# Loading q, k and v head by head in 1 KB pieces, and turning them by fp32 matmuls in blocks of 64 columns

## The chip, the cores and the metric

The kernel runs on one core of a Trainium2 chip. The metric is the device time of one execution in microseconds, the median of several runs. The engines of the core are TensorE (PE in the profile; its weight loads are shown apart as PEld), VectorE (DVE), ScalarE (ACT), GpSimd (POOL) and SyncE (SP, which here only issues DMAs). They run their own instruction lists in order and wait for one another by semaphores.

## The reference

Attention that keeps the 32 largest scores of each row, and behind it a feed-forward layer with a squared ReLU. The shapes are 8 batches, 8 heads, 576 rows, 64 columns for q, k and v, and 512 to 2048 to 512 for the layer; all inputs and the output are fp32.

```
scores = q @ k.T / 8                                  # per batch and head, 576 x 576
kth    = 32nd largest of each row
attn   = exp(scores - max) where scores >= kth, else 0; each row divided by its sum
x      = attn @ v                                     # heads put side by side: 4608 x 512
out    = relu(x @ w_in) ** 2 @ w_out
```

## The kernel before

**Tiling.** Two heads of one batch make a pair; there are 32 pairs. The 576 rows of a head are cut into 4 chunks of 128 (row `4 p + c` stands on partition `p` of chunk `c`) and a remainder of 64. A step `u` handles 128 query rows of two heads at once, against all 576 keys; the remainders of two pairs share two steps. There are 144 steps, in an order written out in `steps`.

**One step.** TensorE makes the scores in two banks of 2 x 288 columns, `sc_a` and `sc_b` (L263, fp32; the two heads of a pair sit on partitions 0 to 63 and 64 to 127 and use the upper and the lower rows of the array). ScalarE copies both banks to `s` (L266). VectorE takes pairwise maxima out of the banks and of `s` (L282, L283, and L285 in the first 20 steps), then maxima and minima of these (L291, L292), and in four rounds the 8 largest values and their removal (L342, L346). From step 20 on VectorE writes one of the pairwise results into the bank `sc_b`, ScalarE copies it out to `most` (L298), and L291 and L292 follow. L292 is the last reader of bank `sc_b`, so the next step's scores for that bank come after it. GpSimd builds the remaining candidates (L307, L316) and a mask (L378), which from step 20 on a DMA issued by GpSimd adds to `s` (L382, `s<-gone`). ScalarE takes the exponentials (L386), a transposing DMA on SyncE's queue turns them (L395, `wT<-w_two`), TensorE multiplies by v (L422), VectorE inverts the row sums (L436), ScalarE scales the result into `x_tok` or `x_rem` (L452, L459). Between these TensorE does pieces of the feed-forward layer, `dense` (L533, L556; L572 are idle pieces), which ScalarE evacuates (L538, L544, L561).

**Preparing a pair.** Each pair has a list of units, `prep_units`: `main` for q, `main` for k, `rest`, `values`. A unit `main` turns the four chunks of two heads with four 128-column transposes of TensorE into one bank `gen` (L161), and ScalarE copies it to `qkT` (L162), for q with the scale. `rest` turns the remainders (L197) and copies them (L199, L200, L202). `values` copies v into bf16 (L206, L209). The first pair is cut up in `first_step` and `first_q` so that the first scores come early. In the main loop one unit is issued per step (two in the first 8 steps, no unit in a step that keeps `values` for later): TensorE's list has it right behind the step's scores, ScalarE's list right behind the copies of these scores.

The order of a step around the change:

```
scores(u + 1)
both(u + 1)
...
prepare(u)
place(u - 4)
exps(u - 2, 0); exps(u - 2, 1); turn(u - 2)
fetch(10 if u < 8 else 3)
topk(u, (1, 2))
pairs_of(u + 1); copy_far(u + 1); lesser(u + 1)
topk(u, (3,))
```

ScalarE's list thus runs: copies of the scores (L266), the copy of a prepared unit (L162 or others), L452 or L459, the exponentials (L386), then `most` (L298), then the feed-forward evacuations.

**Loading.** `load_pair` puts a pair's ten loads into a list, and `fetch` issues them from it on SyncE's queue, ten per step in the first 8 steps and then three: for each of q, k and v one load for each head (L104, rows 0 to 511, 128 KB) and one for the remainder of both (L109, 32 KB), for v twice. The tile is `[128, 5, 2, 64]`: chunk, head, column, so that a chunk of both heads is a run of 128 columns for the transpose, and each load writes pieces of 64 fp32 (256 bytes). The tiles have two buffers. `load_first` does the same for the first pair on SyncE's and ScalarE's queues (L131, L134).

Of the kernel before, what the change touches and what calls it, by code (L numbers as in the profile page):

```python
# [13 lines left out]
f32 = mybir.dt.float32  # L14
# [4 lines left out]
AF = mybir.ActivationFunctionType  # L19
# [4 lines left out]
def kernel(  # L24
# [9 lines left out]
    nc = tc.nc  # L34
# [10 lines left out]
    def pin(ins):  # L45
        tc.keep_in_program_order(ins)
        return ins
# [3 lines left out]
    ld = fast.enter_context(tc.tile_pool(name="ld", bufs=2))  # L51
# [9 lines left out]
    id_f = const.tile([128, 128], f32, name="id_f")  # L61
# [30 lines left out]
    raw, prep = {}, {}  # L92

    fetches = []

    def load_pair(i):
        b, pr = pairs[i]
        raw[i] = [None] * 3

        def whole_rows(z, name, two, a):  # L100
            def go():
                if a == 0:
                    raw[i][z] = ld.tile([128, 5, 2, 64], f32, name=name)
                pin(nc.sync.dma_start(out=raw[i][z][:, 0:4, a, :], in_=two[a, 0:512].rearrange("(p c) d -> p c d", c=4)))  # L104
            return go

        def rest_rows(z, two, at):
            def go():
                pin(nc.sync.dma_start(out=raw[i][z][at:at + 64, 4], in_=two[:, 512:576].rearrange("h p d -> p h d")))  # L109
            return go  # L110

        for z, (name, src) in enumerate((("q_raw", q), ("k_raw", k), ("v_raw", v))):
            two = src[b, 2 * pr:2 * pr + 2]
            for a in range(2):
                fetches.append((i, whole_rows(z, name, two, a)))
            fetches.append((i, rest_rows(z, two, 0)))
            if z == 2:
                fetches.append((i, rest_rows(z, two, 64)))

    def fetch(n):  # L120
        while n and fetches:
            fetches.pop(0)[1]()
            n -= 1


    def load_first():
        raw[0] = [ld.tile([128, 5, 2, 64], f32, name=name) for name in ("q_raw", "k_raw", "v_raw")]
        at = [z[0, 0:2] for z in (q, k, v)]

        def rows(queue, z, a):  # L130
            pin(queue.dma_start(out=raw[0][z][:, 0:4, a, :], in_=at[z][a, 0:512].rearrange("(p c) d -> p c d", c=4)))  # L131

        def last(queue, z, to=0):
            pin(queue.dma_start(out=raw[0][z][to:to + 64, 4], in_=at[z][:, 512:576].rearrange("h p d -> p h d")))  # L134

        for z in (1, 0):
            rows(nc.sync, z, 0)
            rows(nc.scalar, z, 1)
        last(nc.sync, 1)
        last(nc.scalar, 0)  # L140
        rows(nc.sync, 2, 0)
        rows(nc.sync, 2, 1)
        last(nc.sync, 2)
        last(nc.sync, 2, 64)

    def prep_units(i):
        q_raw, k_raw, v_raw = raw[i]
        qkT = heads.tile([128, 512 + 640], f32, name="qkT")
        qT, kT = qkT[:, 0:512], qkT[:, 512:1152]
        k_rest = kT.rearrange("p (n d) -> p n d", d=64)[:, 0:10:9]  # L150
        bd, va = qbd[i % 5], vau[i % 6]
        prep[i] = (qT, kT, bd, va)

        def twice(t):
            return t.rearrange("p (o d) -> p o d", o=1).broadcast_to([128, 2, 64])

        def main(which, src):
            def go():
                tp = ps_one.tile([128, 512], f32, name="gen", bufs=2)
                for c in range(4):  # L160
                    pin(nc.tensor.transpose(tp[:, c * 128:(c + 1) * 128], src[:, c], id_f[:, :]))  # L161
                pin(nc.scalar.activation((qT, kT[:, 64:576])[which], tp[:, :], AF.Copy, scale=(scale, 1.0)[which]))  # L162
            return go


        def first_step():
            for j, bank in ((0, "gen"), (1, "gen"), (2, "dn_ps"), (3, "sc_a")):
                if bank == "sc_a":
                    tp = ps_sc.tile([128, 2, 512], f32, name=bank)[:, 0, :]
                else:  # L170
                    tp = ps_one.tile([128, 512], f32, name=bank, bufs=2 if bank == "gen" else None)
                if j < 2:
                    for c in range(2):
                        pin(nc.tensor.transpose(tp[:, c * 128:(c + 1) * 128], k_raw[:, 2 * j + c], id_f[:, :]))
                    to, got = kT[:, 64 + j * 256:64 + (j + 1) * 256], tp[:, 0:256]
                elif j == 2:
                    pin(nc.tensor.transpose(tp[:, 0:128], q_raw[:, 0], id_f[:, :]))
                    to, got = qT[:, 0:128], tp[:, 0:128]
                else:
                    pin(nc.tensor.transpose(tp[:, 0:64], k_raw[0:64, 4], id_f[0:64, 0:64]))  # L180
                    to, got = k_rest, twice(tp[:, 0:64])
                if j % 2:
                    pin(nc.vector.tensor_copy(to, got))
                else:
                    pin(nc.scalar.activation(to, got, AF.Copy, scale=scale if j == 2 else 1.0))

        def first_q():
            tp = ps_one.tile([128, 512], f32, name="gen", bufs=2)
            for c in range(1, 4):
                pin(nc.tensor.transpose(tp[:, c * 128:(c + 1) * 128], q_raw[:, c], id_f[:, :]))  # L190
            pin(nc.scalar.activation(qT[:, 128:512], tp[:, 128:512], AF.Copy, scale=scale))

        def rest(both=(0, 1)):
            tp = ps_one.tile([128, 512], f32, name="gen", bufs=2)
            for which in both:
                src = (q_raw, k_raw)[which]
                pin(nc.tensor.transpose(tp[:, which * 64:(which + 1) * 64], src[0:64, 4], id_f[0:64, 0:64]))  # L197
            if 0 in both:
                pin(nc.scalar.activation(bd[0:64, 0:64], tp[0:64, 0:64], AF.Copy, scale=scale))  # L199
                pin(nc.scalar.activation(bd[64:128, 64:128], tp[64:128, 0:64], AF.Copy, scale=scale))  # L200
            if 1 in both:
                pin(nc.scalar.activation(k_rest, twice(tp[:, 64:128]), AF.Copy))  # L202

        def values():
            assert i < 6 or av_left[i - 6] == 0
            pin(nc.scalar.activation(va[:, 0:4, :, 0:64], v_raw[:, 0:4], AF.Copy))  # L206
            for x in range(2):
                half = slice(64 * x, 64 * x + 64)
                pin(nc.scalar.activation(va[half, 4 + x, :, 0:64], v_raw[half, 4], AF.Copy))  # L209
# [418 lines left out]


    load_first()  # L630
    load_pair(1)
    fetch(10)
    soon, coming = prep_units(0), 1
    soon.pop(0)()

# [34 lines left out]
    def ok(w):  # L670
        return 0 <= w < U
# [16 lines left out]
    for u in range(U):  # L688
        for x in range(2):
            if ok(u - 1) and not by_vector(u - 1, x):  # L690
                drop(u - 1, x)
        quads_of(u)
        topk(u, (0,))
        if ok(u - 4):
            invert(u - 4)
        if ok(u + 1):
            for i, c, a in steps[u + 1]:
                while coming <= i or (coming == i + 1 and soon):
# [198 lines left out]
```

## Time and profile before

| | us |
|---|---|
| median of the runs | 942.67 |
| lowest, highest of 3 | 941.9, 949.06 |
| the profiled execution | 951.19 |
| its span, first to last instruction | 949.4 |
| busy TensorE, weight loads | 685.4, 413.2 |
| busy VectorE | 897.8 |
| busy ScalarE | 785.9 |
| busy GpSimd | 777.3 |

The profile comes from one execution. A row of the timeline gives start and duration in us, engine, line, operation, output and input, and how many instructions were merged; in brackets stands how long the engine was idle before it and for whom it waited. A row of the list of waits gives engine and line, whom it waited for, the total in us, how often, and the longest. A row of the groups gives the count, then busy us and mean ns, then idle time before the group. A row of the windows gives the window, its length, busy time and count of each engine, and last the clock granted to TensorE, the busy share of the DMA engines and GB/s.

### The profile page before, as it was taken

What the parts mean: (1) busy time and instruction counts of PE and PEld (TensorE: products, weight loads), DVE (VectorE), ACT (ScalarE), POOL (GpSimd) and SP (SyncE); (2) the same over time, 40 slices, a digit from 0 to 9 for tenths busy, and PEclk for the clock granted to TensorE, in tenths of its full rate; (3) what the DMA queues carried; (4) which work ended last, traced back from release to release, by engine and by line L of the source; (5) the groups of instructions that cost most, each with busy time, mean ns of one, the idle gap of its engine ahead of it and who ended that gap; (6) DMA issues with size and microseconds to landing.
All of it is one profiled execution on the core that took longest, in us unless ns stands there. A gap on an engine that the chain in (4) does not pass through costs nothing.

```text
span 949.4 us, 19099 instructions
## 1 busy us (share of the span) xinstructions
PE 685.4 (72%) x5264; PEld 413.2 (44%) x5264; DVE 897.8 (95%) x3635; ACT 785.9 (83%) x1778; POOL 777.3 (82%) x803
## 2 busy tenths in 40 slices
PE   6777677777677777667766677777777777688766
PEld 3333344445354434344544434444544443455544
DVE  5999999999899999999979999999999999999971
ACT  4677897888698979798969888889899987988982
POOL 7888889887788898988878888888888888898850
PEclk9998988997889999998879999999899999998999
DMA  5667866898999999989899999898999999687741
GB/s 138 131 157 173 172 131 131 180 195 183 175 189 177 193 218 185 208 180 192 189 150 194 191 205 212 185 197 185 193 204 198 196 199 214 141 174 159 159 110 38
DMA packets 329969, 166.16 MB, mean 175 GB/s; under 512 B 306560, under 2 KB 306560, under 8 KB 329856
## 3 DMA queue, kind: packets, MB, share of 16 engines
q1 hardware_dynamic: 311088, 92.62, 51.3%
q0 software_dynamic: 17568, 71.97, 33.3%
q8 instruction: 44, 0.72, 0.3%
q14 instruction: 69, 0.57, 0.2%
q10 hardware_dynamic: 1200, 0.30, 0.1%
HBM read 37.75 MB, written 9.44 MB: 50 GB/s over the span
## 4 chain that ended last, share of the span: by engine, by line
DVE 49%; issue 10%; ACT 7%; DMA 7%; POOL 5%; PE 4%; SPq 0%; POOLq 0%; ACTq 0%
DVE m L342 20%; DVE cat L346 14%; DMA s<-gone_b 5%; DVE sc_b L282 4%; DVE cat L291 4%; DVE cat L292 4%; DVE most L283 3%; PE dn_ps L556 2%; DMA s<-gone_a 1%; PE gen L533 1%; POOL cat L316 1%; POOL gone_b L378 1%; POOL gone_a L378 1%; ACT w_two_c L386 1%; DVE rsum L436 1%
## 5 line engine op out<-in xcount | busy, mean ns | idle before, releaser
L342 DVE MAX8 m<-cat 128x8 f32<-128x104 f32 (+3 forms) x1152 | 446.9, 430 | 0.0
L346 DVE MATCH_REPLACE8 cat<-m,cat 128x104 f32<-128x104 f32 (+2 forms) x864 | 270.7, 322 | 0.0
L307 POOL TENSOR_TENSOR cat<-s 128x576 int32<-128x576 int32 (+1 forms) x144 | 230.5, 1601 | 2.9 <-ACT s L266 2.9
L316 POOL TENSOR_TENSOR cat<-cat,most 128x576 int32<-128x576 int32 (+1 forms) x144 | 190.2, 1321 | 28.6 <-ACT most L298 8.8
L263 PE MATMUL sc_b<-qkT 64*128 64x288 f32 x512 | 108.1, 497 | 125.3 <-DVE cat L292 123.5
L556 PE MATMUL dn_ps<-w_out,h 128*128 128x512 bf16 x576 | 162.0, 417 | 3.6 <-ACT wide L561 3.6
L533 PEld LDWEIGHTS <-w_in 128*128 128x128 bf16 x1408 | 126.6, 105 | 70.1 <-issue 38.2
L533 PE MATMUL gen<-xT,w_in 128*128 128x256 bf16 (+1 forms) x1120 | 140.2, 277 | 15.4 <-ACT qkT L202 5.9
L266 ACT ACTIVATE s<-sc_b 128x576 f32<-128x576 f32 x144 | 93.3, 648 | 61.4 <-PE sc_b L263 60.5
L378 POOL TENSOR_SCALAR gone_b<-s,neg 128x576 uint8<-128x576 f32 x142 | 106.0, 746 | 32.5 <-ACT neg L361 22.9
L378 POOL TENSOR_SCALAR gone_a<-s,neg 128x576 uint8<-128x576 f32 x143 | 106.7, 746 | 29.4 <-ACT neg L361 20.6
L263 PE MATMUL sc_a<-qkT 64*128 64x288 f32 x512 | 102.6, 477 | 31.0 <-DVE most L283 21.0
L263 PEld LDWEIGHTS sc_b<-qkT 64*128 64x128 f32 x512 | 46.8, 205 | 177.9 <-issue 95.7
L266 ACT ACTIVATE s<-sc_a 128x576 f32<-128x576 f32 x144 | 91.6, 636 | 11.5 <-PE sc_a L263 10.5
L422 PEld LDWEIGHTS <-wT 128*128 128x128 bf16 (+1 forms) x1600 | 61.7, 102 | 85.3 <-DMA wT<-w_two_b 31.9
L538 ACT ACTIVATE rl<-gen 128x512 f32<-128x512 f32 x142 | 84.7, 597 | 12.6 <-PE gen L533 12.1
L544 ACT ACTIVATE h<-rl 128x512 bf16<-128x512 f32 x138 | 86.9, 630 | 4.4
L556 PEld LDWEIGHTS <-h 128*128 128x128 bf16 x576 | 56.1, 105 | 70.6 <-issue 32.9
L386 ACT ACTIVATE w_two_c<-s,neg 128x576 bf16<-128x576 f32 x94 | 68.0, 780 | 16.0 <-DMA s<-gone_b 12.1
L291 DVE TENSOR_TENSOR cat<-sc_b,most 128x288 f32<-128x288 f32 x144 | 63.8, 443 | 13.4 <-ACT most L298 13.2
L386 ACT ACTIVATE w_two_b<-s,neg 128x576 bf16<-128x576 f32 x95 | 68.8, 780 | 3.9 <-DMA s<-gone_b 2.4
L382 POOL DMA_DIRECT2D s<-gone_b x61 | 54.2, 888 | 20.1 <-DVE cat L346 7.4
(165 smaller groups left out, 1202.0 us busy)
## 6 DMA issues: line engine op xcount, KB each, us to landing
s<-gone_a POOLq DMA_DIRECT2D x61, 576.0 KB, 4.7
s<-gone_b POOLq DMA_DIRECT2D x61, 576.0 KB, 4.7
v_raw<-in_v_dram SPq DMA_DIRECT2D x64, 128.0 KB, 3.2
out_dram<-wide SPq DMA_DIRECT2D x32, 256.0 KB, 2.7
k_raw<-in_k_dram SPq DMA_DIRECT2D x63, 128.0 KB, 3.3
q_raw<-in_q_dram SPq DMA_DIRECT2D x63, 128.0 KB, 3.0
wide<-in_moe_w_in_dram SPq DMA_DIRECT2D x8, 512.0 KB, 4.3
wide<-in_moe_w_out_dram SPq DMA_DIRECT2D x8, 512.0 KB, 4.2
```

The lines of the kernel that those rows point to most:

```text
L263: pin(nc.tensor.matmul(out=ps[j][:, x, 0:HALF], lhsT=lhsT, rhs=rhs, start=True, stop=True))
L266: pin(nc.scalar.activation(s[:, :, j * HALF:(j + 1) * HALF], ps[j][:, :, 0:HALF], AF.Copy))
L291: pin(tt(cat[:, :, 0:QUAR], far, near, op=ALU.max))
L307: pin(tt(less, s[:, :, 0:wide].bitcast(i32), s[:, :, HALF:HALF + wide].bitcast(i32), op=ALU.add))
L316: pin(tt(less, less, d["most"][:, 0:n_h, :, :].bitcast(i32).rearrange("p h x n -> p x h n"), op=ALU.subtract))
L342: pin(nc.vector.max(out=m[r][:, x, :], in_=part(r, x)))
L346: pin(nc.vector.match_replace(out=part(r, x), in_to_replace=m[r][:, x, :], in_values=part(r, x), imm_value=NEG))
L378: pin(nc.gpsimd.tensor_scalar(byte[:, x, :, 1], s[:, x, :], scalar1=d["neg"][:, x, 1:2], scalar2=-HUGE, op0=ALU.add, op1=ALU.mult))
L386: pin(nc.scalar.activation(w_two[u % 3][:, x, 0:S], d["s"][:, x, :], AF.Exp, bias=d["neg"][:, x, 0:1]))
L533: pin(nc.tensor.matmul(out=hp[:, n * n_rows:(n + 1) * n_rows], lhsT=w_in[:, kh, (f0 + n) * 128:(f0 + n + 1) * 128], rhs=xt(kh), start=(kh ...
L544: pin(nc.scalar.activation(h2, flat, AF.Square))
L556: pin(nc.tensor.matmul(out=op[:, :], lhsT=held["h2"][:, f, c * 128:(c + 1) * 128], rhs=w_out[:, f, :], start=(f == 0), stop=(f == NF - 1)))
```

## The change

The tile of raw rows becomes `[128, 640]`: on each partition first the 4 rows of one head (256 columns, 1 KB), then those of the other, then 128 columns for the remainder of both. One load now brings rows 0 to 511 of both heads, and its pieces are 1 KB long, on both sides. A pair has seven loads; `fetch` issues seven in the first steps and then two. The first pair's loads keep their number and their queues and are 1 KB in their pieces as well.

A chunk of both heads is no longer one run of columns. The new function `flip` turns it by two ordinary fp32 matmuls: the 64 columns of one head are the weights, the identity is the moving operand (128 columns), and the results go to partitions 0 to 63 and 64 to 127 of the bank. `main`, `first_step` and `first_q` use it. The remainders keep the transpose. `values` reads v in another order.

```
+    def rest_of(t, at):
+        return t[at:at + 64, 512:640].rearrange("p (h d) -> p h d", h=2)
+
+    def flip(to, t, c):
+        for a in range(2):
+            pin(nc.tensor.matmul(out=to[64 * a:64 * a + 64, :], lhsT=t[:, 256 * a + 64 * c:256 * a + 64 * c + 64], rhs=id_f[:, :], start=True, stop=True))
...
-        def whole_rows(z, name, two, a):
+        def whole_rows(z, name, two):
             def go():
-                if a == 0:
-                    raw[i][z] = ld.tile([128, 5, 2, 64], f32, name=name)
-                pin(nc.sync.dma_start(out=raw[i][z][:, 0:4, a, :], in_=two[a, 0:512].rearrange("(p c) d -> p c d", c=4)))
+                t = raw[i][z] = ld.tile([128, 640], f32, name=name)
+                pin(nc.sync.dma_start(out=t[:, 0:512].rearrange("p (h x) -> p h x", h=2), in_=two[:, 0:512].rearrange("h (p c) d -> p h (c d)", c=4)))
...
-            pin(queue.dma_start(out=raw[0][z][:, 0:4, a, :], in_=at[z][a, 0:512].rearrange("(p c) d -> p c d", c=4)))
+            pin(queue.dma_start(out=raw[0][z][:, 256 * a:256 * a + 256], in_=at[z][a, 0:512].rearrange("(p c) d -> p (c d)", c=4)))
...
                 for c in range(4):
-                    pin(nc.tensor.transpose(tp[:, c * 128:(c + 1) * 128], src[:, c], id_f[:, :]))
+                    flip(tp[:, c * 128:(c + 1) * 128], src, c)
                 pin(nc.scalar.activation((qT, kT[:, 64:576])[which], tp[:, :], AF.Copy, scale=(scale, 1.0)[which]))
...
-            pin(nc.scalar.activation(va[:, 0:4, :, 0:64], v_raw[:, 0:4], AF.Copy))
+            pin(nc.scalar.activation(va[:, 0:4, :, 0:64], v_raw[:, 0:512].rearrange("p (a c d) -> p c a d", a=2, c=4), AF.Copy))
...
-    fetch(10)
+    fetch(7)
...
-        fetch(10 if u < 8 else 3)
+        fetch(7 if u < 8 else 2)
```

More of the change, by code (lines that the diff above doesn't have):

```diff
@@ L108, in go @@
             def go():
-                pin(nc.sync.dma_start(out=raw[i][z][at:at + 64, 4], in_=two[:, 512:576].rearrange("h p d -> p h d")))
+                pin(nc.sync.dma_start(out=rest_of(raw[i][z], at), in_=two[:, 512:576].rearrange("h p d -> p h d")))
             return go
@@ L113, in load_pair @@
             two = src[b, 2 * pr:2 * pr + 2]
-            for a in range(2):
-                fetches.append((i, whole_rows(z, name, two, a)))
+            fetches.append((i, whole_rows(z, name, two)))
             fetches.append((i, rest_rows(z, two, 0)))
@@ L126, in load_first @@
     def load_first():
-        raw[0] = [ld.tile([128, 5, 2, 64], f32, name=name) for name in ("q_raw", "k_raw", "v_raw")]
+        raw[0] = [ld.tile([128, 640], f32, name=name) for name in ("q_raw", "k_raw", "v_raw")]
         at = [z[0, 0:2] for z in (q, k, v)]
         def rows(queue, z, a):
-            pin(queue.dma_start(out=raw[0][z][:, 0:4, a, :], in_=at[z][a, 0:512].rearrange("(p c) d -> p c d", c=4)))
+            pin(queue.dma_start(out=raw[0][z][:, 256 * a:256 * a + 256], in_=at[z][a, 0:512].rearrange("(p c) d -> p (c d)", c=4)))
         def last(queue, z, to=0):
-            pin(queue.dma_start(out=raw[0][z][to:to + 64, 4], in_=at[z][:, 512:576].rearrange("h p d -> p h d")))
+            pin(queue.dma_start(out=rest_of(raw[0][z], to), in_=at[z][:, 512:576].rearrange("h p d -> p h d")))
         for z in (1, 0):
@@ L173, in first_step @@
                     for c in range(2):
-                        pin(nc.tensor.transpose(tp[:, c * 128:(c + 1) * 128], k_raw[:, 2 * j + c], id_f[:, :]))
+                        flip(tp[:, c * 128:(c + 1) * 128], k_raw, 2 * j + c)
                     to, got = kT[:, 64 + j * 256:64 + (j + 1) * 256], tp[:, 0:256]
                 elif j == 2:
-                    pin(nc.tensor.transpose(tp[:, 0:128], q_raw[:, 0], id_f[:, :]))
+                    flip(tp[:, 0:128], q_raw, 0)
                     to, got = qT[:, 0:128], tp[:, 0:128]
                 else:
-                    pin(nc.tensor.transpose(tp[:, 0:64], k_raw[0:64, 4], id_f[0:64, 0:64]))
+                    pin(nc.tensor.transpose(tp[:, 0:64], k_raw[0:64, 512:640], id_f[0:64, 0:64]))
                     to, got = k_rest, twice(tp[:, 0:64])
@@ L189, in first_q @@
             for c in range(1, 4):
-                pin(nc.tensor.transpose(tp[:, c * 128:(c + 1) * 128], q_raw[:, c], id_f[:, :]))
+                flip(tp[:, c * 128:(c + 1) * 128], q_raw, c)
             pin(nc.scalar.activation(qT[:, 128:512], tp[:, 128:512], AF.Copy, scale=scale))
@@ L196, in rest @@
                 src = (q_raw, k_raw)[which]
-                pin(nc.tensor.transpose(tp[:, which * 64:(which + 1) * 64], src[0:64, 4], id_f[0:64, 0:64]))
+                pin(nc.tensor.transpose(tp[:, which * 64:(which + 1) * 64], src[0:64, 512:640], id_f[0:64, 0:64]))
             if 0 in both:
@@ L205, in values @@
             assert i < 6 or av_left[i - 6] == 0
-            pin(nc.scalar.activation(va[:, 0:4, :, 0:64], v_raw[:, 0:4], AF.Copy))
+            pin(nc.scalar.activation(va[:, 0:4, :, 0:64], v_raw[:, 0:512].rearrange("p (a c d) -> p c a d", a=2, c=4), AF.Copy))
             for x in range(2):
                 half = slice(64 * x, 64 * x + 64)
-                pin(nc.scalar.activation(va[half, 4 + x, :, 0:64], v_raw[half, 4], AF.Copy))
+                pin(nc.scalar.activation(va[half, 4 + x, :, 0:64], rest_of(v_raw, 64 * x), AF.Copy))
         if i == 0:
```

## The prediction

> **What bounds the kernel now.** I read the page's busy shares first, then the list of waits, then the timeline of one step.
>
> ```profile
> PE 685.4 (72%) x5264; PEld 413.2 (44%) x5264; DVE 897.8 (95%) x3635; ACT 785.9 (83%) x1778; POOL 777.3 (82%) x803
> ```
>
> VectorE (DVE) is busy 897.8 of 949.4 us. Whatever makes it wait costs time one for one; whatever merely relieves another engine gains at most what VectorE now waits for. The list of waits says for what:
>
> ```profile
> PE sc_b L263 <- DVE cat L292: 130.5, 121, 2.9
> ACT s L266 <- PE sc_b L263: 60.5, 76, 1.8
> DVE cat L291 <- ACT most L298: 13.2, 10, 5.0
> ACT qkT L162 <- PE gen L161: 3.8, 10, 0.4
> ```
>
> TensorE waits 130.5 us for VectorE ahead of the second score bank, ScalarE 60.5 us for that bank, and VectorE in turn 13.2 us for ScalarE's copy `most`. That is a ring: DVE L292, scores, copy of the scores, ScalarE's list, `most`, DVE L291. One turn of it, in a step that also prepares q of a pair:
>
> ```profile
> 407.33 0.45 DVE L292 TENSOR_TENSOR cat<-sc_b,most 128x288 f32<-128x288 f32 x1
> ...
> 407.93 0.76 PE L263 MATMUL sc_b<-qkT 64*128 64x288 f32 x4 [1.29 <-DVE cat L292]
> ...
> 408.62 0.66 PE L161 MATMUL gen<-id_f,q_raw 128*128 128x128 f32 x4
> ...
> 408.72 0.65 ACT L266 ACTIVATE s<-sc_b 128x576 f32<-128x576 f32 x1 [0.88 <-PE sc_b L263]
> ...
> 409.31 0.60 ACT L162 ACTIVATE qkT<-gen 128x512 f32<-128x512 f32 x1
> ...
> 409.80 1.26 ACT L459 ACTIVATE x_rem_b<-av_ps,rsum 64x64 bf16<-64x64 f32 x4
> ...
> 411.02 0.46 DVE L282 TENSOR_TENSOR sc_b<-sc_a,s 128x288 f32<-128x288 f32 x1
> 411.09 1.44 ACT L386 ACTIVATE w_two_a<-s,neg 128x576 bf16<-128x576 f32 x2
> ...
> 412.56 0.41 ACT L298 ACTIVATE most<-sc_b 128x288 f32<-128x288 f32 x1
> ...
> 413.07 0.44 DVE L291 TENSOR_TENSOR cat<-sc_b,most 128x288 f32<-128x288 f32 x1
> ```
>
> From 408.72 to 412.97 ScalarE runs without a gap. The four transposes end at 409.28 and their copy L162 starts at 409.31; `most` ends at 412.97 and VectorE takes it at 413.07. So the transposes lie on this ring with 0.03 us to spare at their copy and 0.1 us at VectorE. TensorE as a whole has room (72%); at this place it has none.
>
> The two largest stalls come from a DMA instead:
>
> ```profile
> 258.15 1.44 ACT L386 ACTIVATE w_two_c<-s,neg 128x576 bf16<-128x576 f32 x2 [5.52 <-DMA s<-gone_b]
> ...
> 259.92 0.46 DVE L291 TENSOR_TENSOR cat<-sc_b,most 128x288 f32<-128x288 f32 x1 [3.91 <-ACT most L298]
> ...
> 484.46 1.44 ACT L386 ACTIVATE w_two_c<-s,neg 128x576 bf16<-128x576 f32 x2 [6.58 <-DMA s<-gone_b]
> ...
> 486.23 0.46 DVE L291 TENSOR_TENSOR cat<-sc_b,most 128x288 f32<-128x288 f32 x1 [4.97 <-ACT most L298]
> ```
>
> The accumulating DMA on `s` landed late, `most` stood behind the exponentials that need it, and VectorE lost 3.91 + 4.97 = 8.9 of the 13.2 us.
>
> **The change part by part.** *The turning.* Each pair has two main units (q and k), 64 in all; the first pair's are cut up in `first_step` and `first_q`, the other 62 are L161 and L162. A unit goes from four 128-column transposes to eight fp32 matmuls by the identity, 64 columns of weights and 128 moving columns each, into the upper and lower half of one bank. The price of such a matmul has to come from other rows:
>
> ```profile
> L161 PE MATMUL gen<-id_f,q_raw 128*128 128x128 f32 x124 | 25.8, 343 | 0.0
> ```
>
> ```profile
> 400.42 0.65 PE L263 MATMUL sc_a<-qkT,qbd_a 128*128 128x288 f32 x2
> ...
> 400.66 0.41 PE L263 MATMUL sc_a<-qkT,qbd_a 128*128 128x288 f32 x1
> ...
> 403.74 1.04 PE L533 MATMUL gen<-xT,w_in 128*128 128x256 bf16 x8
> ...
> 404.70 0.37 PE L422 MATMUL av_ps<-vau_a,wT 128*64 128x65 bf16 x9
> ...
> 404.92 0.35 PE L422 MATMUL av_ps<-vau_b,wT 128*64 128x65 bf16 x9
> ...
> 411.12 0.46 PE L422 MATMUL av_ps<-vau_b,wT 128*128 128x65 bf16 x10
> ```
>
> The group shows that a transpose is one record (31 units of q with four each). The timeline shows that an ordinary fp32 matmul is two: of the one at 400.42 the second record (the same view, cut to it) starts at 400.66, 0.24 us behind the first, and lasts 0.41, so 0.41 - 0.24 = 0.17 us is its tail. 0.24 us for 288 columns is 0.107 us for 128, so a new matmul takes 0.213 us of the array. If the two halves of a block run side by side, a unit is 4 x 0.213 + 0.17 = 1.02 us; one after the other, 8 x 0.213 + 0.17 = 1.87 us. Against the 0.66 us of now that is +0.36 or +1.2.
>
> Two rows speak for side by side. The score matmuls at 407.93, which split the array by rows, put two 288-column products into 0.76 us, where one whole one takes 0.65 and two in turn would take 1.13. And the weighting matmuls of 64 columns (128*64) split it by columns: of a step's twenty the first starts at 404.70 and the last ends at 405.27, 0.57 us where ten whole ones take 0.46. In turn, at (0.46 - 0.17) / 9 = 0.03 us apiece, they would take 19 x 0.03 + 0.17 = 0.74. I take side by side with a little lost at each of the four blocks, as the score pair lost 0.11 over the ideal 0.65: **+0.5 us** for a unit. Ends: +0.36 and +1.2.
>
> The Trainium skill speaks against this part: "TensorE: Matmul & The Clock Gate", section Terms, calls transpose mode four times faster for fp32, and "TensorEngine Tiling (Array Packing)", section Restrictions, excludes that mode under column tiling. By that rule alone four transposes' spacing would grow fourfold to about 1.9 us, the serial end of the range.
>
> What lies on the path? ScalarE's copy waits for the last of the eight, so the delay goes down ScalarE's list to `most`, less the cover at each place. I went through the 50 main units from 143 us on (in the first 20 steps L298 is not issued, so this wait cannot arise; I take nothing for the 12 units there, at the far end 12 x 0.5 = 6 us). Cover is what the copy lags behind the transposes, plus ScalarE's gaps up to `most`, plus what VectorE leaves between `most` and L291.
>
> ```profile
> 185.81 0.41 ACT L298 ACTIVATE most<-sc_b 128x288 f32<-128x288 f32 x1
> ...
> 186.34 0.43 DVE L291 TENSOR_TENSOR cat<-sc_b,most 128x288 f32<-128x288 f32 x1
> ...
> 188.39 1.11 PE L161 MATMUL gen<-id_f,k_raw 128*128 128x128 f32 x4
> ...
> 417.88 0.43 ACT L298 ACTIVATE most<-sc_b 128x288 f32<-128x288 f32 x1
> ...
> 419.17 0.44 DVE L291 TENSOR_TENSOR cat<-sc_b,most 128x288 f32<-128x288 f32 x1
> ...
> 776.22 1.11 PE L161 MATMUL gen<-id_f,q_raw 128*128 128x128 f32 x4
> ...
> 779.59 0.41 ACT L298 ACTIVATE most<-sc_b 128x288 f32<-128x288 f32 x1
> ...
> 780.10 0.46 DVE L291 TENSOR_TENSOR cat<-sc_b,most 128x288 f32<-128x288 f32 x1
> ...
> 803.98 0.41 ACT L298 ACTIVATE most<-sc_b 128x288 f32<-128x288 f32 x1
> ...
> 804.49 0.45 DVE L291 TENSOR_TENSOR cat<-sc_b,most 128x288 f32<-128x288 f32 x1
> ```
>
> Thirteen units of 0.66 us are tight, like those of the first and the last pair of rows (186.34 - 186.22 = 0.12, 804.49 - 804.39 = 0.10; mean 0.11). Four have about 0.47. Twenty-one are loose, mean 1.04, like the pair at 417.88 (0.86 us, and the copy lagged by another 0.26). Twelve units take 1.11 us, the first at 188.39 and the last at 776.22: TensorE runs them at about half rate. Ten of these have 0.09 us of cover, two 0.68. For a slow unit the addition is about twice: 1.7 + 0.2 = 1.9, up to 2.0 against 1.11, so **+0.9**. The sum: 13 x 0.39 + 4 x 0.03 + 0 + 10 x 0.81 + 2 x 0.22 = **+14 us**. At the low end (+0.36, slow +0.7) it is 13 x 0.25 + 10 x 0.61 = +9; serial (+1.2, slow +2.4) 13 x 1.09 + 4 x 0.73 + 21 x 0.16 + 10 x 2.31 + 2 x 1.72 = +47.
>
> Behind the flips TensorE's queue holds the dense pieces, the weighting products and the next first score bank. They shift by the same 0.5, and the 1.29 us for which TensorE stands ahead of the second bank takes it up; were that gone, it would cost 0.5 us in each of 62 units.
>
> *The loads.* Pieces of 256 bytes become 1 KB, ten loads of a pair seven, three per step two.
>
> ```profile
> 3.00:5.00 2.00, 0.76 (x4) 0.71 (x4) 0.00 (x0) 1.16 (x2) 2.00 (x2) 1.00 1.05 234
> ...
> 21.00:22.00 1.00, 0.94 (x5) 0.29 (x3) 1.00 (x6) 0.99 (x4) 0.92 (x2) 1.00 0.84 311
> ```
>
> With only 256-byte loads under way the DMA engines are full at 234 GB/s (the last two columns are share and GB/s); with a weight load beside them they move 311 at 0.84, or 370 full. 256 KB take 1.12 us by the one and at least 0.71 by the other: up to 0.4 us less DMA time in each load step. What that is worth is the late `s<-gone_b`, and it is not clear that the loads made it late. Bounds: 0, and all 13.2 us. I take half of the 8.9: **-4.5 us**; a unit that holds VectorE up also gives GpSimd and DMA time to catch up, which works the same way. The 92 loads fewer free SyncE, which waits for ScalarE anyway: nothing. The transposing DMAs behind the loads in SyncE's queue can only start sooner.
>
> *`values` and the remainders.* ScalarE reads v in 64-element pieces in another order, as many elements; L266 copies two pieces of 288 in 0.65 us for 576, no more for the split: nothing. `rest` keeps its transposes.
>
> *The head.*
>
> ```profile
> 4.24 1.08 PE L174 MATMUL gen<-id_f,k_raw 128*128 128x128 f32 x4 [4.24 <-DMA k_raw<-in_k_dram]
> ...
> 6.27 0.45 PE L177 MATMUL dn_ps<-id_f,q_raw 128*128 128x128 f32 x1 [0.95 <-DMA q_raw<-in_q_dram]
> ```
>
> The first k blocks take 0.8 us longer, the q block perhaps 0.2; but TensorE waits for q until 6.27, and the loads, faster by up to a third, may bring q up to 1 us sooner. I take 0, ends -1 and +1.
>
> The sum is +14 - 4.5 = +9.5 us on the profiled execution's own 951.19 us (span 949.4). The median of the runs shown, 942.67, lies 8.5 below it, so most runs presumably lack some stall of the trace, and the DMA part may be smaller there. Put onto the median: 942.67 + 9.5 = **952 us**. About 1% is what a measurement here can tell from no change, so this lies at that border.
>
> **The rivals.** *1. The halves do not overlap* (fp32 splitting by columns occurs nowhere in this trace). Then +47 - 4.5: 985 us, 965 to 990.
>
> *2. The DMA part wins, not slower than before.* One mechanism: at the DMA engines, the shorter loads stop the late landings of `s<-gone`. Price 13.2 us; with the flips at their low end, 13.2 - 9 = 4 us faster, 939. It decides once the loads explain more than 9 of the 13.2 us. For it: both big stalls follow a step with v loads. Against it: 0.4 us a load step is little beside landings about 5 us late.
>
> *3. Switching drains the array.* If the flips must wait until the scores are out (0.17 us of tail, twice that at half rate), the tight units cost 13 x 0.17 + 10 x 0.34 = 6 us more: 958. "TensorEngine Tiling (Array Packing)", section Key Properties, in the Trainium skill says that changing the tiling mode drains TensorE. Rows disagree for other switches: the transposes start at 408.62 with the scores in flight until 408.69, and the 64-column matmuls at 404.70 with L533 in flight until 404.78.
>
> **How the numbers follow.** Forecast 0.45 (945 to 962, a little less than half within 1%), serial 0.20, DMA wins 0.24 (a third of it below 933), drain 0.11. Faster by over 1%: 0.08. Within: 0.20 + 0.16 + 0.04 = 0.40. Slower: 0.25 + 0.20 + 0.07 = 0.52. The range, 938 to 980, leaves out the upper part of the serial case and the lowest of the DMA case.
>
> **What would show it.** Right: L167's copies of the changed kernel wait for the flips in some 35 places instead of 10, the flips span about 1.2 us warm, and L296 waits for `most` some 25 times more, by 0.3 to 0.9 us. Wrong: flips of 1.9 us (rival 1), or DMA waits of ScalarE gone from the list and L291's wait at its successor below 10 us in total (rival 2); a VectorE busy time other than 898 us would break the whole frame.

## The result and the profile after

The changed kernel takes **953.67 us** (median of 14 runs, 947.86 to 966.28) against 944.22 (14 runs, 939.44 to 951.27) of the kernel before, a ratio of **1.0083 [1.0054, 1.0113]**: slower by 0.8%, or some 8 us. A ratio compares the runs without single slow ones (of after the one of 966.28 us, below two of one experiment), so it is not the quotient of the two medians. The profiled execution of after took 954.81 us, span 953.0.

The busy shares of after, from the page (TensorE's 768 instructions more are the new matmuls, VectorE's work is what it was):

```profile
PE 705.2 (74%) x6032; PEld 433.5 (45%) x6032; DVE 899.0 (94%) x3635; ACT 787.5 (83%) x1778; POOL 779.0 (82%) x803
```

The list of waits of after (engine and line, what it waited for; us in total, times, the longest):

```profile
PE sc_b L268 <- DVE cat L297: 143.4, 122, 3.0
...
ACT s L271 <- PE sc_b L268: 50.1, 61, 1.8
...
ACT qkT L167 <- PE gen L101: 24.2, 46, 1.3
...
DVE cat L296 <- ACT most L303: 15.5, 23, 1.9
```

ScalarE's copy of the turned rows now waits in 46 places instead of 10, and VectorE waits for `most` 23 times instead of 10. The sum of the last row rose only from 13.2 to 15.5 us, because the two stalls of 3.91 and 4.97 us behind `s<-gone_b` are not in this execution.

One turn of the ring in the timeline of after (start, length, in brackets the idle time ahead), beside which the step at 407.93 of before can be held:

```profile
206.32 0.76 PE L268 MATMUL sc_b<-qkT 64*128 64x288 f32 x4 [1.29 <-DVE cat L297]
207.00 1.09 PE L101 MATMUL gen<-id_f,q_raw 128*64 128x128 f32 x16
207.11 0.65 ACT L271 ACTIVATE s<-sc_b 128x576 f32<-128x576 f32 x1 [0.88 <-PE sc_b L268]
208.15 0.60 ACT L167 ACTIVATE qkT<-gen 128x512 f32<-128x512 f32 x1 [0.38 <-PE gen L101]
208.64 1.26 ACT L464 ACTIVATE x_rem_b<-av_ps,rsum 64x64 bf16<-64x64 f32 x4
...
209.93 1.44 ACT L391 ACTIVATE w_two_b<-s,neg 128x576 bf16<-128x576 f32 x2
...
211.40 0.41 ACT L303 ACTIVATE most<-sc_b 128x288 f32<-128x288 f32 x1
...
211.84 0.46 DVE L296 TENSOR_TENSOR cat<-sc_b,most 128x288 f32<-128x288 f32 x1 [0.29 <-ACT most L303]
```

The eight fp32 matmuls (16 records, as forecast) take 1.09 us instead of 0.66: in the two traces the starts of consecutive transposes lie 0.11 us apart, those of consecutive blocks of the flips 0.22, and there are four blocks. The copy L167 starts 0.38 us late, ScalarE's list behind it moves as a whole, and VectorE loses 0.29 us at L296. This is the chain that the prediction drew.

To count it over the whole execution I took the distance from one DVE L282 (L287 in after) to the next. From the 20th on it is 6.10 us where nothing is in the way. What lies above that adds up to 17.4 us before, nearly all of it in 15 steps, and to 20.7 us in 27 steps after. Two of the 15 are the DMA stalls, 4.00 and 5.05 us of excess. Without them it goes from 8.4 to 20.7: **+12.3 us** of small delays. Of the 27, ten are below 0.5 us, fourteen of 0.5 to 1.2 and three of 1.7 to 2.0.

### The profile page after: what moved, and what is told of

Same layout as the page of the kernel before. It is cut to its first block, busy times and chain, and to the rows that moved or that the text cites. A ratio compares the mean times of both kernels' runs of the same rounds, so it can differ in the third digit from the quotient of the medians.

```text
span 953.0 us, 20498 instructions
## 1 busy us (share of the span) xinstructions
PE 705.2 (74%) x6032; PEld 433.5 (45%) x6032; DVE 899.0 (94%) x3635; ACT 787.5 (83%) x1778; POOL 779.0 (82%) x803
## 4 chain that ended last, share of the span: by engine, by line
DVE 53%; issue 10%; ACT 9%; PE 6%; DMA 2%; POOL 2%; SPq 0%; ACTq 0%; POOLq 0%
DVE m L347 22%; DVE cat L351 15%; DVE sc_b L287 4%; DVE cat L296 4%; DVE cat L297 4%; DVE most L288 3%; ACT w_two_a L391 2%; PE dn_ps L561 2%; PE gen L101 1%; ACT most L303 1%; PE gen L538 1%; ACT w_two_b L391 1%; PE sc_b L268 1%; DMA s<-gone_a 1%; DVE rsum L441 1%
## 5 line engine op out<-in xcount | busy, mean ns | idle before, releaser
L268 PE MATMUL sc_b<-qkT 64*128 64x288 f32 x512 | 105.4, 485 | 137.4 <-DVE cat L297 134.2
L561 PE MATMUL dn_ps<-w_out,h 128*128 128x512 bf16 x576 | 155.9, 405 | 3.6 <-ACT wide L566 3.6
L538 PEld LDWEIGHTS <-w_in 128*128 128x128 bf16 x1408 | 121.5, 102 | 64.8 <-issue 35.5
L538 PE MATMUL gen<-xT,w_in 128*128 128x256 bf16 (+1 forms) x1120 | 135.9, 271 | 13.4 <-ACT qkT L207 8.4
L271 ACT ACTIVATE s<-sc_a 128x576 f32<-128x576 f32 x144 | 91.6, 636 | 11.1 <-PE sc_a L268 10.5
L561 PEld LDWEIGHTS <-h 128*128 128x128 bf16 x576 | 51.0, 102 | 75.3 <-issue 36.9
L296 DVE TENSOR_TENSOR cat<-sc_b,most 128x288 f32<-128x288 f32 x144 | 63.8, 443 | 15.5 <-ACT most L303 15.5
```

Of the source, the lines that this page charges most:

```text
L268: pin(nc.tensor.matmul(out=ps[j][:, x, 0:HALF], lhsT=lhsT, rhs=rhs, start=True, stop=True))
L271: pin(nc.scalar.activation(s[:, :, j * HALF:(j + 1) * HALF], ps[j][:, :, 0:HALF], AF.Copy))
L296: pin(tt(cat[:, :, 0:QUAR], far, near, op=ALU.max))
L538: pin(nc.tensor.matmul(out=hp[:, n * n_rows:(n + 1) * n_rows], lhsT=w_in[:, kh, (f0 + n) * 128:(f0 + n + 1) * 128], rhs=xt(kh), start=(kh ...
L561: pin(nc.tensor.matmul(out=op[:, :], lhsT=held["h2"][:, f, c * 128:(c + 1) * 128], rhs=w_out[:, f, :], start=(f == 0), stop=(f == NF - 1)))
```

## The experiments

In the kernels that turn 128 columns of the new layout, a turned block holds two chunks of one head instead of one chunk of two, so scores are made of other pairs of rows than the reference asks for; the count and shape of all instructions stay as they were. These are the loads alone (twice), the ten loads, the three with additional loads or moved transposes on top of them. The others compute what the reference does.

**The two parts apart.** *The loads alone*: the layout and the seven loads of the change, turned as before.

```
-        for a in range(2):
-            pin(nc.tensor.matmul(out=to[64*a:64*a+64, :], lhsT=t[:, 256*a+64*c:256*a+64*c+64], rhs=id_f[:, :], ...))
+        pin(nc.tensor.transpose(to, t[:, 128*c:128*c+128], id_f[:, :]))
```

> The loads of the changed kernel (1 KB pieces, seven per pair) with the four 128-column transposes of the kernel before. A run of 128 columns now holds two chunks of one head, not one chunk of both heads, so q and k rows are paired otherwise and the output is that of another pairing; every instruction has the same shape as before. Theory A (the turning costs, the loads gain): transposes 0.66 us warm, ScalarE's copy waits for them about 10 times as before, the many 0.3 us waits of VectorE for `most` are gone, the two DMA stalls of 3.9 and 5.0 us at steps 39 and 75 stay away; ratio to the kernel before 0.992 to 1.000. Theory B (the larger loads cost, because 256 KB stand in SyncE's queue ahead of the turning DMA; the flips are hidden, TensorE being 74% busy): ratio about 1.008, and VectorE's waits for `most` as in the changed kernel, 23 times.

*The turning alone*: tile and ten loads of before, eight matmuls a unit (`lhsT=t[:, c, a]`).

> The loads of the kernel before (256-byte pieces, ten per pair) with the changed turning (two fp32 matmuls of 64 columns a block). Theory A: warm units 1.09 us, about 25 waits of VectorE for `most` more; the cover counted from the trace of before with +0.43 us warm and +0.86 slow gives +12 us, ratio 1.010 to 1.015, larger than the 1.0083 of the whole change. Theory B: ratio 0.998 to 1.002.

Measured: loads alone 939.94 us, ratio 0.9959 [0.9932, 0.9987]; turning alone 956.42, ratio 1.0111 [1.0067, 1.0155]. The turning is the loss, and it shows the waits of after nearly row for row (25 waits for `most` in all; the expectation had about 25 more than the 10 of before). The waits of the kernel with the turning alone:

```profile
ACT qkT L166 <- PE gen L98: 25.5, 48, 1.3
...
DVE cat L295 <- ACT most L302: 14.2, 25, 1.7
```

The loads looked like a small gain; that number is taken up again below.

**Is it the split into halves?** Before's loads, and one whole 128-column fp32 matmul for each block instead of two halves.

```
+    def flip(to, t, c):
+        pin(nc.tensor.matmul(out=to, lhsT=t[:, c], rhs=id_f[:, :], start=True, stop=True))
...
-                    pin(nc.tensor.transpose(tp[:, c * 128:(c + 1) * 128], src[:, c], id_f[:, :]))
+                    flip(tp[:, c * 128:(c + 1) * 128], src, c)
```

> As the turning alone, with one ordinary fp32 matmul of 128 columns a block in place of two of 64 (loads of the kernel before). If the two halves run side by side, the whole blocks take as long: unit 1.02 to 1.1 us, ratio as the turning alone within 0.3%. If the splitting by columns itself costs (a drain at the switch, lost overlap), the unit falls below 0.9 us and the ratio falls by half of the turning's.

Measured: 959.31 us, ratio 1.0164 [1.0108, 1.022]. Two units in its timeline, one where TensorE runs at full rate and one where it runs at about half:

```profile
323.93 1.16 PE L97 MATMUL gen<-id_f,q_raw 128*128 128x128 f32 x8
330.46 2.07 PE L97 MATMUL gen<-id_f,k_raw 128*128 128x128 f32 x8
```

Four whole blocks (8 records) take 1.16 us, eight halves 1.09. So the halves run side by side and the split costs nothing; the price is that of an ordinary fp32 matmul in place of a transpose. Both numbers lie a little above what was expected for this case (1.02 to 1.1 us, and a ratio within 0.3% of 1.0111): a whole block is somewhat dearer than two halves, and why was not looked for.

**Is it the place on the ring?** After, with the flips of a main unit issued twice; and after, with them issued between the score matmuls of the first bank and those of the second, where TensorE waits for VectorE anyway.

```
                 for c in range(4):
                     flip(tp[:, c * 128:(c + 1) * 128], src, c)
+                for c in range(4):
+                    flip(tp[:, c * 128:(c + 1) * 128], src, c)
```

> The changed kernel with the eight matmuls of every main unit issued twice into the same bank, all else equal. Theory A (what counts is by how much a unit outlasts its cover on the ring to `most`): a unit goes to 1.95 us warm and 3.7 slow, +1.29 and +2.6 over the transposes, which eats the loose places too (mean cover 1.04); the cover counted from the trace of before gives +52 us over the kernel before with the loads' gain still off, ratio 1.03 to 1.06. Rival C (TensorE's time as such costs, in proportion): twice the turning's 1.1%, ratio about 1.02. Rival D (a fixed price of the switch of shapes): no more than the turning alone, 1.011.

```
-    def scores(u):
+    def scores(u, between=None):
...
+            if between and j == js[1]:
+                between()          # the flips; their copy stays where it was
...
-            scores(u + 1)
+            scores(u + 1, early)   # early: the next main unit's flips, from the ninth step on
```

> The changed kernel with the matmuls of a main unit issued between the scores of the first and of the second bank, where TensorE waits 1.29 us for VectorE; ScalarE's copy stays where it was. Theory A: ScalarE's copy no longer waits for the flips (24 us in 46 waits becomes under 5), the waits of VectorE for `most` fall below those of the kernel before, and the ratio is 0.985 to 1.000. If the second bank's scores are pushed out instead (a unit of 1.09 us in a gap of 1.29, of 1.97 where the clock is low), some waits come back behind L271, ratio 1.000 to 1.005. Theory B: no change from 1.008.

Measured: turned twice 996.53 us, ratio **1.0547 [1.0499, 1.0596]**, that is +51.8 us; the cover table of the prediction, with three times the measured addition (1.29 us, and 2.57 at half rate; a unit of twice the flips takes 1.97 us), gives 13 x 1.18 + 4 x 0.82 + 21 x 0.25 + 10 x 2.48 + 2 x 1.89 = +52.5. That rules out both rivals, a cost in proportion to TensorE's time (1.02) and a fixed price of the switch (1.011). How close the two numbers come is partly luck. By the count of steps from above this trace has, from the 20th step on, 54.4 us of excess against the 8.4 of before, that is 46.0 more, some 4 of them from a late `s<-gone_a`; another 5.1 us fall into the first 20 steps, which the table leaves out. Its waits:

```profile
ACT qkT L169 <- PE gen L101: 81.3, 60, 3.0
DVE cat L298 <- ACT most L305: 43.2, 31, 5.4
```

Between the banks: 948.78 us, ratio 1.0016 [0.9981, 1.005]. The flips are as long as in after, but their result is ready when ScalarE comes to copy it, and the copy waits in 6 places instead of 46. Its timeline at the step of the prediction, and its waits:

```profile
400.11 1.09 PE L101 MATMUL gen<-id_f,q_raw 128*64 128x128 f32 x16
...
401.48 0.76 PE L278 MATMUL sc_b<-qkT 64*128 64x288 f32 x4 [0.27 <-DVE cat L307]
...
402.27 0.65 ACT L281 ACTIVATE s<-sc_b 128x576 f32<-128x576 f32 x1 [0.88 <-PE sc_b L278]
402.81 0.59 ACT L174 ACTIVATE qkT<-gen 128x512 f32<-128x512 f32 x1
```

```profile
DVE cat L306 <- ACT most L313: 8.9, 10, 2.3
...
ACT qkT L174 <- PE gen L101: 3.0, 6, 1.3
```

TensorE's wait ahead of the second bank shrank from 1.29 to 0.27 us: the flips use it up. So the cost is that of the place, not of the work: the ratio falls from 1.0083 to 1.0016 when the same matmuls stand one place earlier. The count of steps agrees: 16.0 us of excess, 5.1 of them in one step near 787 us in which ScalarE waits 3.91 us for `s<-gone_a`; the other 11.0 stand against 20.7 in after and 8.4 before. The ratio is above the 0.985 to 1.000 that was expected; it lies in the range named for the case that the second bank's scores are held up a little.

*The transposes of before in that place*, to see whether the kernel before also paid there:

> The kernel before with the four transposes of a main unit issued between the scores of the first and of the second bank. Theory A: the 10 waits of ScalarE's copy (3.8 us) go, and with them the short waits of VectorE for `most` behind prepared units (about 1.5 us in the trace of before); ratio 0.996 to 1.000, and less gain than the same move brought to the changed kernel (0.7%).

Measured: 943.93 us, ratio 0.999 [0.9956, 1.0023]. ScalarE's copy now waits in 2 places instead of 10, but that gains nothing that the ratio can tell from no change (0.4% at most). Before had the 0.03 us to spare that the prediction read.

**What the loads are worth.** The prediction gave them 4.5 us for longer pieces. The next kernel is the loads alone with 1 KB pieces but ten loads a pair, three a step, as before.

```
...
-            fetches.append((i, whole_rows(z, name, two)))     # both heads, 256 KB
+            for a in range(2):
+                fetches.append((i, whole_rows(z, name, two, a)))   # one head, 128 KB
...
```

> As the loads alone, with the pieces of 1 KB but ten loads a pair, one for each head, three per step (output again that of another pairing). If the length of the pieces brings the loads' gain: ratio 0.994 to 0.998, as with seven loads. If the number of loads brings it: 0.999 to 1.002.

Measured: 944.01 us, ratio 0.9999 [0.9972, 1.0025], with 256241 DMA packets instead of before's 329969. The longer pieces alone bring nothing that the ratio can show. Two waits of VectorE stand in most traces with ten loads and in few with seven, one near 61 us and one near 215 us. So the next theory was SyncE's queue: each load takes it some 0.6 us to issue, and transposing DMAs stand behind. Three kernels on one chip went after that, the loads alone with three additional loads of 4 bytes, the loads alone once more, and the loads alone with the transposes between the banks:

```
             fetches.append((i, whole_rows(z, name, two)))
+            fetches.append((i, small_load(z, two)))      # 4 bytes into rows of the q or k tile that nobody reads
...
-        fetch(7 if u < 8 else 2)
+        fetch(10 if u < 8 else 3)
```

> The loads-alone kernel with three loads of four bytes more for each pair (into a place that nobody reads), so that SyncE issues ten loads a pair and three a step again, while the bytes and the 1 KB pieces stay. Theory (what the loads gave comes from SyncE's queue: each issue takes 0.6 us, and the transposing DMAs of the weights stand behind it): the gain of 0.4% goes, ratio 0.998 to 1.002, and the waits of VectorE near 62 us (1.4 to 2.1 us, for ScalarE's s) and in the step near 215 us are back. Rival (the gain comes from fewer, larger transfers in the DMA engines; an issue of four bytes costs nothing there): 0.994 to 0.997 as the loads alone, and no such waits.

> The loads-alone kernel again beside it, on the same chip. If its 0.9959 is no matter of the chip or the day: 0.994 to 0.998, no waits of VectorE at 62 and 215 us. A large stall of ScalarE for the accumulating DMA on s may fall at any step of the trace, or at none.

> The loads of the change, turned by 128-column transposes, which are issued between the two score banks (from the ninth step on). If the two parts act on their own: the loads' 0.996 times the moved transposes' 0.999, so 0.993 to 0.998, and ScalarE's copy of the turned rows waits for TensorE in fewer than ten places. If moving the transposes sets free what the loads then need: below 0.993.

Measured: ten issues 940.65 us, ratio 0.9985 [0.9963, 1.0008]; loads again 942.48, **0.9995 [0.9966, 1.0024]**; loads with moved transposes 943.32, 1.0 [0.997, 1.0029]. The 0.9959 of the first measurement did not come back, and the product of the two parts (0.993 to 0.998 expected) did not either. The waits of VectorE did stay away with the loads alone. The ten issues did not bring them back, so this expectation of the theory failed; but an issue of 4 bytes held SyncE for 0.33 us, not 0.6. The last kernel therefore made the three loads dear (64 pieces of 256 bytes each, 0.5 us):

```
-                pin(nc.sync.dma_start(out=raw[i][min(z, 1)][p:p + 1, 512:513], in_=two[0, 0:1, 0:1]))
+                pin(nc.sync.dma_start(out=raw[i][min(z, 1)][64:128, x:x + 64], in_=two[0, 512:576]))
```

> As the kernel with three small loads more for each pair, but each of the three now takes 64 pieces of 256 bytes (into a place that nobody reads), so that its issue should hold SyncE about 0.6 us like a real load, not 0.33 us as the load of four bytes did. Theory (a queue of ten issues at 0.6 us ends later than ScalarE has the weights, and the transposing DMA behind it comes late): near 50 us the transposing DMA of w_two_a is issued at 50 us or later, over 1 us behind the exponentials that made its source, TensorE waits 3 us or more for it instead of 1.2 to 2.2, and VectorE's wait of 1.4 to 2.1 us near 61 us is back. Rival (it is the large transfers themselves that delay the transposing DMA, not their issue): it is issued by 49.2 us or within 0.6 us of its source, and VectorE does not wait there. The whole time can tell little of 2 to 3 us: 0.996 to 1.002 by either.

Measured: 942.15 us, ratio 0.9973 [0.9944, 1.0003]. Its timeline:

```profile
46.52 1.44 ACT L397 ACTIVATE w_two_a<-s,neg 128x576 bf16<-128x576 f32 x2
...
49.88 1.34 SPq L406 DMA_TRANSPOSE wT<-w_two_a  x1
...
56.07 0.73 PE L433 MATMUL av_ps<-vau_a,wT 128*128 128x65 bf16 x10 [3.82 <-DMA wT<-w_two_a]
...
58.67 1.17 PE L274 MATMUL sc_b<-qkT,qbd_c 128*128 128x288 f32 x2
59.63 1.17 PE L274 MATMUL sc_b<-qkT,qbd_d 128*128 128x288 f32 x2
61.52 0.47 DVE L293 TENSOR_TENSOR sc_b<-sc_a,s 128x288 f32<-128x288 f32 x1 [2.00 <-ACT s L277]
```

and that of the loads alone, second measurement, at the same work:

```profile
47.09 1.44 ACT L390 ACTIVATE w_two_a<-s,neg 128x576 bf16<-128x576 f32 x2
...
49.02 1.38 SPq L399 DMA_TRANSPOSE wT<-w_two_a  x1
...
55.04 0.73 PE L426 MATMUL av_ps<-vau_a,wT 128*128 128x65 bf16 x10 [2.22 <-DMA wT<-w_two_a]
...
57.64 0.88 PE L267 MATMUL sc_b<-qkT,qbd_c 128*128 128x288 f32 x2
58.36 0.65 PE L267 MATMUL sc_b<-qkT,qbd_d 128*128 128x288 f32 x2
59.73 0.47 DVE L286 TENSOR_TENSOR sc_b<-sc_a,s 128x288 f32<-128x288 f32 x1
```

Here the theory holds, place and size (only the issue itself came at 49.88 and not at 50 or later): the transposing DMA is issued 49.88 - 47.96 = 1.92 us behind its source instead of 49.02 - 48.53 = 0.49, TensorE stands still for 3.82 us instead of 2.22 and comes back at about half rate, the scores are late, and VectorE loses 2.00 us. By the same two rows the lag is 0.03 to 0.49 us in the kernels without that wait (the loads alone twice, the three small loads, the moved transposes with the new loads, after, its flips between the banks), and 1.05 to 2.41 us in those that have it, which are the six traces with ten loads of before's kind or of 1 KB, this one, and the flips issued twice. The flips issued twice have seven loads: there one load of v takes 1.59 us to issue instead of 0.59, and the queue ends late all the same.

The size of this can be read from one step. From one first maximum of VectorE to the next (DVE L282 in before, shown with that of the loads alone) the eighth step takes 62.15 - 54.16 = 7.99 us in before and 59.73 - 53.19 = 6.54 without the wait:

```profile
54.16 0.45 DVE L282 TENSOR_TENSOR sc_b<-sc_a,s 128x288 f32<-128x288 f32 x1
62.15 0.47 DVE L282 TENSOR_TENSOR sc_b<-sc_a,s 128x288 f32<-128x288 f32 x1 [1.45 <-ACT s L266]
```

```profile
53.19 0.47 DVE L286 TENSOR_TENSOR sc_b<-sc_a,s 128x288 f32<-128x288 f32 x1
59.73 0.47 DVE L286 TENSOR_TENSOR sc_b<-sc_a,s 128x288 f32<-128x288 f32 x1
```

It is 6.46 to 6.54 us in all six traces without the wait and 7.99 to 9.46 in the eight with it, so the place costs some 1.5 us or more. The other wait is not explained by this: near 215 us the transposing DMA is issued 0.03 us behind its source in every trace, with ten loads too. The longer pieces show at the head instead: with the transposes of before the first DVE L282 comes at 8.96 to 9.54 us in the six traces with 1 KB pieces and at 10.21 to 10.50 in the three with 256-byte pieces, about 1 us earlier. Each of these effects is smaller than what a ratio resolves: the kernel with the dear loads, which has the waits, came out at 0.9973, below its sister without them (0.9995). For the loads as a whole, the four kernels with 1 KB pieces and the transposes in their place, one of them twice (0.9959, 0.9995, 0.9999, 0.9985, 0.9973), average 0.9982: about **-1.7 us**, where each ratio is uncertain by 0.3%.

**Which stalls belong to an execution, not to a kernel?** Before, profiled a second time:

> The kernel before once more, for a second trace. If the two stalls of 3.9 and 5.0 us at steps 39 and 75 belong to the kernel, they are there again; if they are chance, they are elsewhere or gone, and then no single trace can credit the loads with their absence.

Measured: 951.46 us, span 949.7. The excess near 259 us is there again (4.41 instead of 4.00 us), the one near 486 us (5.05) is gone, and one of 3.52 us stands near 810 us. A stall of this kind, 5.0 us long, also lies in the second trace of the loads alone and none in its first; the kernel with the dear loads has one of 5.5 us near 259 us again, with 1 KB pieces. So they come and go between executions of one kernel, more often at some places than at others, and the 1 KB pieces do not remove them. What makes `s<-gone` late was not found.

No kernel here beats both; the lowest, the loads with 128-column transposes, leave the reference's pairing.

## Why the prediction was right

**The forecast of 952 us and +1% held (953.67; +0.8%), and its larger term by the chain it named. Its smaller term, the loads, failed, and that the sum came out as close as it did is partly luck.** Point by point:

- *VectorE sets the time, and the ring closes over `most`.* Right. VectorE's busy time stayed at 899.0 (898 forecast), and the kernels that lengthen the flips or move them off the ring move the time as the ring says.
- *A unit takes +0.5 us.* Right in kind, a little high: +0.43 at the full clock, 1.97 - 1.11 = +0.86 at half rate (+0.9 forecast). Next to nothing is lost at the four blocks; the middle of the two ends was the safe choice, not the exact one.
- *The cover of 50 units, +14 us.* The table with the measured lengths (+0.43 and +0.86) gives 13 x 0.32 + 10 x 0.77 + 2 x 0.18 = +12.2 us, the trace +12.3, the turning alone 1.0111, or +10.5 [6.3, 14.6]. One count was off: twelve late units were taken as slow, in the trace of after eight are. Turning twice shows that the table has the right size at three times the delay too, though it gives some 6 to 10 us more than the trace has in the steps that it covers.
- *The 12 units of the first 20 steps: nothing.* Wrong by about 2 us. `most` is indeed not awaited there, but VectorE's first 20 steps take 131.7 us with the turning alone against 129.2 before, and 129.3 in after against 127.7 with the loads alone. The flips reach VectorE by another way, which was not followed up.
- *Loads -4.5 us by half of the large stalls.* The step that failed. The term was too large (-1.7 on average) and its reason wrong: longer pieces alone gave 0.9999, and the stalls it counted on come and go without the change. "92 loads fewer: nothing" was too short as well: in the eighth step SyncE's queue, with ten issues ahead of a transposing DMA, reaches VectorE and costs it 1.5 us or more. Both terms of the sum were too large, by some 2 and 3 us with opposite signs, so that the sum came out closer than its parts.
- *Head: 0.* About right. The first DVE L282 comes at 9.80 us instead of 10.50 and 10.21 in the two traces of before; the loads alone bring it to 9.02 and 9.54, the turning alone leaves it at 10.43.
- *Values and remainders: nothing.* No new wait of theirs shows in the list.
- *Rival 1, serial halves (985).* Out: 1.09 us, not 1.87.
- *Rival 2, the DMA part wins (939).* Out, with its mechanism: the loads alone cannot be told from no change in the second measurement. Of its signs, the large DMA stalls did go from the list of after, but the second trace of before shows that they do so by themselves; the wait of VectorE for `most` did not fall below 10 us (15.5).
- *Rival 3, a drain at the switch (958).* Out. The flips of after start 0.68 us behind the scores (207.00, 206.32), the transposes of before 0.69 us (408.62, 407.93), both while the scores are in flight by the timeline (until 207.08 and 408.69). The rule of the Trainium skill ("TensorEngine Tiling (Array Packing)", section Key Properties) that a change of tiling mode drains TensorE shows no price here beyond that of the switch from the scores to the transposes, which before has too.
- *What would show it.* The order of size came, not the counts: the copies of the changed kernel wait in 46 places (35 forecast), a unit takes 1.09 us (1.2), and VectorE waits for `most` 23 times, 0.28 to 1.93 us long, which is 13 times more than before (25 times more forecast, by 0.3 to 0.9 us).

The serial end of the range, which the prediction set beside rules of the Trainium skill, did not come either: a block of flips follows the last one after 0.22 us, a transpose after 0.11, which is twice and not four times, and a unit went from 0.66 to 1.09 us. The Trainium skill ("TensorE: Matmul & The Clock Gate", section Terms) calls transpose mode four times faster for fp32; for units of four blocks this case does not agree. No run tries the other rule named there, that column tiling excludes this mode (the Trainium skill, "TensorEngine Tiling (Array Packing)", section Restrictions).

## What to carry to other kernels

An engine with 26% idle time can still cost the full length of what it does at one place: look for the slack at that place, in hundredths of a microsecond, and first try whether the added work fits into a wait that the same engine has anyway (here the 1.29 us ahead of the second score bank). A forecast by counting cover place by place held here for 0.4 us of delay, and in size for 1.3 us, and is worth the effort; but count the places ahead of the steady steps too. A stall of 5 us in one profiled execution is no budget: profile the same kernel a second time before crediting a change with removing it.

## What was not expected of the hardware

- **The granted clock of TensorE differs with what it is given, and not by the number of flips**: 0.941 in the trace of after against 0.922 before; as a mean over runs 0.944 with the turning alone (6 runs) against 0.930 of before beside it (23 runs). But the flips issued twice give 0.932 (4 runs) against 0.926 of before beside them (23 runs), four whole blocks 0.934 (4 runs) against 0.930, and before with its transposes moved between the banks 0.934 (12 runs) against 0.926. Fewer units of after ran slow (eight instead of twelve), which fits. What raises the clock was not tried.
- **Eight fp32 halves are no dearer than four whole blocks**: 1.09 against 1.16 us. Either takes two records a block where a transpose takes one.
- **The price of an issue on SyncE's queue hardly follows its bytes.** In the timeline of the kernel with three small loads, the issues of 256 KB (L109), of 4 bytes (L115) and of 32 KB in pieces of 256 bytes (L120):

```profile
44.02 0.54 SPq L109 DMA_DIRECT2D k_raw<-in_k_dram  x1
44.61 0.31 SPq L115 DMA_DIRECT2D k_raw<-in_k_dram  x1
44.97 0.60 SPq L120 DMA_DIRECT2D k_raw<-in_k_dram  x1
```

  The ten loads of a pair take 6.6 us in the early steps of before (44.23 to 50.83), longer than a step there (6.46 us).
